# Products of an attention stage cut into half-width pieces for TensorE's array, on one core

## The chip, the cores and the metric

The kernel runs on one core of a Trainium2 chip. The core has TensorE (PE in the profile, its weight loads as PEld), VectorE (DVE), ScalarE (ACT), GpSimd (POOL) and SyncE (SP, which issues DMAs). The metric is the device time of one execution in microseconds. Before the change it is 1563.07 us, the median of three runs (1562.79 to 1563.94).

## The reference

Attention with a decaying state gives x, and x goes through a mixture of eight experts. Per batch b and head h (4 batches, 8 heads, 768 tokens, head size 48):

```
for t in range(S):
    cur   = (u * k[t]) outer v[t]
    y[t]  = r[t] @ (state + cur)
    state = w[:, None] * state + k[t] outer v[t]
x = y, as 3072 tokens x 384
P = exp(x @ w_gate - max), 8 rounds of row and column normalisation
out = sum over e of P[:, e] * (relu(x @ w1[e]) @ w2[e])
```

The inputs are float32. `w1` is 384 x 1024 and `w2` is 1024 x 384 for each expert.

## The kernel before

The first part of the program is a loop over 24 chunks of 128 tokens (`i` in line 733, six chunks to a batch, `c = tt % NCHB`). All of its attention products are float32. For one chunk it holds these stages, each a function:

- `prep` scales r on POOL (`rp`) and k on DVE (`kp`) by tables of powers of w. The heads are stored 64 wide, 48 used and 16 zero, so that two heads (a "pair") fill 128 columns; there are four pairs.
- `stage_b` transposes `rp` and `kp` on PE (`prT`, `pkT`) and ACT copies them out (`rT`, `kT`).
- `stage_c` makes the scores `pA` (eight products, each over 64 of the array's 128 rows), which DVE copies under a mask into `at`; and the chunk's addition to the state, `pu` (four products, `kp` of a pair as weights, 128 x 128, v of the pair streamed, 96 columns). Only the two 48 x 48 blocks on the diagonal of a pair's result are wanted; the table `wbd` holds the decay there and zero elsewhere. DVE adds the old state `S`, and POOL multiplies by `wbd`. The last chunk of a batch has no `pu`, the first one no old state.
- `stage_d` makes y in one PSUM bank `py`: with an old state, four products with `rT` of a pair as weights and `S` streamed (96 columns); then eight, one per head, with `at` as weights and v streamed (48 columns). DVE adds the bonus term (`x`), takes the row's maximum and a power of two as scale.
- `stage_e` and `stage_f` transpose x (`px`), split it into two float16 parts and make the gate's logits.

A float32 product stands as two weight loads and two matmuls in the trace.

The loop is a software pipeline: iteration `i` does `prep(i+2)`, `stage_b(i+1)`, `stage_c(i)`, `stage_e(i-2)`, `stage_d(i-1)`, `stage_f(i-3)`. Every engine takes its instructions in the order in which the program issues them (the class `InOrder`, line 21), so the code fixes the order. Between the stages stand two kinds of filler work. `work(n)` puts in units of the first expert (`ph`: x times w1, `po`: h times w2, float16, split into high and low parts); up to `i = 4` it puts in idle matmuls on zeros (`spin`, `pz`). `prepare()` takes the next step of a list: first the splitting of the first expert's weights (maximum, scale, then a high part on ACT and a low part on DVE, `ws`), later sums of token groups for the other experts (rebuild on DVE, additions on POOL, splitting on ACT and DVE, `xv`). The table `STEPS` (line 721) says for each iteration how many such steps stand ahead of `stage_d` and how many behind it. PSUM tiles of the attention come from `ps3`, four banks with one tag.

After the loop come the remaining units and the other seven experts, where PE does float16 products of up to 512 columns until the end. The change touches nothing there.

Of the kernel before, what the change touches and what calls it, by code (L numbers as in the profile page):

```python
# [8 lines left out]
F32 = mybir.dt.float32  # L9
# [3 lines left out]
ALU = mybir.AluOpType  # L13
# [19 lines left out]
def rwkv_sinkhorn_moe(  # L33
# [30 lines left out]
    HP = 64  # L64
# [204 lines left out]
    ac = att.enter_context(tc.tile_pool(name="ac", bufs=1))  # L269
    ld = att.enter_context(tc.tile_pool(name="ld", bufs=3))  # L270
    at2 = att.enter_context(tc.tile_pool(name="at2", bufs=2))
    ps3 = att.enter_context(tc.tile_pool(name="ps3", bufs=4, space=PSUM))
# [69 lines left out]
    def fill(x_):  # L342
        n = x_.shape[1]
        S_.mul(
            x_.rearrange("p (a q) -> p a q", q=HP),
            unit[:, :1, 1:].broadcast_to([P, n // HP, HP]), 0.0,
        )
# [3 lines left out]
    wbd = ac.tile([P, NPAIR, 2, D], F32, name="wbd")  # L351
# [10 lines left out]
    rp_ = [ac.tile([P, H, HP], F32, name=f"rp{i}") for i in range(2)]  # L362
    kp_ = [ac.tile([P, H, HP], F32, name=f"kp{i}") for i in range(3)]
    at_ = [ac.tile([P, H, C], F32, name=f"at{i}") for i in range(2)]
    for t_ in rp_ + kp_:
        G.memset(t_[:, :, D:], 0.0)
    fill(at_[0].rearrange("p h c -> p (h c)"))

    rk0 = at2.tile([P, H, D], F32, tag="rk", name="rk_0", bufs=3)
# [91 lines left out]
    for j in range(2):  # L461
        rows = slice(j * HP, j * HP + D)
# [61 lines left out]
    def stage_c(tt):  # L524
        d = st[tt]
        c = tt % NCHB
        rT, kT = d["rT"], d["kT"]
        at = at_[tt % 2].rearrange("p (a g) c -> p g a c", g=2)
        pas = []
        for g in range(2):  # L530
            pa = ps3.tile([P, NPAIR, C], F32, tag="pa", name=f"pA_{tt}_{g}")
            pas.append(pa)
        for a in range(NPAIR):
            for g in range(2):
                rows = slice(g * HP, g * HP + HP)
                T.matmul(pas[g][:, a, :], kT[rows, a, :], rT[rows, a, :], start=True, stop=True)
        for g in range(2):
            V.copy_predicated(
                at[:, g], maski.unsqueeze(1).broadcast_to([P, NPAIR, C]), pas[g]
            )  # L540
        if c < NCHB - 1:
            vn = loads[tt]["v"]
            kp = kp_[tt % 3].rearrange("p (a j) d -> p a (j d)", j=2)
            pu = ps3.tile([P, NPAIR, 2 * D], F32, tag="pa", name=f"pu_{tt}")
            for p_ in range(NPAIR):
                T.matmul(
                    pu[:, p_, :], kp[:, p_, :],
                    vn[:, 2 * p_ : 2 * p_ + 2, :].rearrange("p j d -> p (j d)"),
                    start=True, stop=True,
                )  # L550
            sn = at2.tile([P, NPAIR, 2 * D], F32, tag="S", name=f"S_{tt}", bufs=3)
            wb = wbd.rearrange("p a j d -> p a (j d)")
            if c == 0:
                V.tensor_tensor(sn, pu, wb, op=ALU.mult)
            else:
                V.tensor_tensor(sn, pu, d["S"], op=ALU.add)
                G.tensor_tensor(sn, sn, wb, op=ALU.mult)
            st.setdefault(("S", tt + 1), sn)

    def stage_d(tt):  # L560
        d = st[tt]
        c = tt % NCHB
        vn = loads[tt]["v"]
        at = at_[tt % 2]
        py = ps3.tile([P, H, D], F32, tag="pa", name=f"py_{tt}")
        pyp = py.rearrange("p (a j) d -> p a (j d)", j=2)
        first = True
        if c > 0:
            for p_ in range(NPAIR):
                T.matmul(pyp[:, p_, :], d["rT"][:, p_, :], d["S"][:, p_, :], start=first, stop=False)  # L570
                first = False
        for h in range(H):
            T.matmul(py[:, h, :], at[:, h, :], vn[:, h, :], start=first, stop=(h == H - 1))
            first = False
        x = at2.tile([P, DM], F32, tag="x", name=f"x_{tt}")
        V.tensor_tensor(x, py.rearrange("p h d -> p (h d)"), d["av"].rearrange("p h d -> p (h d)"), op=ALU.add)
        m = at2.tile([P, 1], F32, tag="xm", name=f"xm_{tt}")
        V.tensor_reduce(m, x, axis=AX.X, op=ALU.max, apply_absolute_value=True)
        s = at2.tile([P, 1], F32, tag="xs", name=f"xs_{tt}")
        pow2_scale(m, inv_s[:, tt : tt + 1], s, 0.125)  # L580
        d["x"], d["s"] = x, s
# [134 lines left out]
    for sg in range(3):  # L716
# [2 lines left out]
        side += steps  # L719

    STEPS = {
        0: (2, 1), 1: (1, 2), 2: (3, 1), 3: (1, 1),
        4: (1, 1), 5: (1, 1), 6: (2, 1), 7: (1, 1), 8: (1, 1),
    }

    def n_steps(i):
# [6 lines left out]
    for i in range(NTT + 3):  # L733
# [15 lines left out]
        if i < NTT:  # L749
            bonus(i)  # L750
            if ("S", i) in st:
                st[i]["S"] = st.pop(("S", i))
            stage_c(i)
# [17 lines left out]
        if 1 <= i <= NTT:  # L771
            stage_d(i - 1)
# [417 lines left out]
    for s in range(NS):  # L1190
        tasks = stage_tasks(s)
        for g in range(NG):
            for j in range(2):
                for n, nxt in enumerate(g1_slots(s, g, j)):
# [3 lines left out]
                    i = j * NPR + n  # L1198
# [37 lines left out]
```

## Time and profile before

| | |
|---|---|
| median of three runs | 1563.07 us |
| the profiled execution, its own time | 1562.66 us |
| its span | 1561.0 us |
| what lies around the span | 1.66 us |
| granted TensorE clock | 1.00 |
| first row of the loop's iterations to the last y product | about 15 to 257 us |

A row of a group shows the engine, the output and inputs, the tile shapes, the number of instructions, the busy time and the mean of one. `128*128` in a PE row is the part of the array in use, rows by columns. A mean of a matmul is its latency, 270 ns and more; matmuls overlap one another, so what a product costs PE is read from the chain of waits, where the pieces add up without overlap.

### The profile page before, as it was taken

What the parts mean: (1) busy time and instruction counts of PE and PEld (TensorE: products, weight loads), DVE (VectorE), ACT (ScalarE), POOL (GpSimd) and SP (SyncE); (2) the same over time, 40 slices, a digit from 0 to 9 for tenths busy, and PEclk for the clock granted to TensorE, in tenths of its full rate; (3) what the DMA queues carried; (4) which work ended last, traced back from release to release, by engine and by line L of the source; (5) the groups of instructions that cost most, each with busy time, mean ns of one, the idle gap of its engine ahead of it and who ended that gap; (6) DMA issues with size and microseconds to landing.
All of it is one profiled execution on the core that took longest, in us unless ns stands there. A gap on an engine that the chain in (4) does not pass through costs nothing.

```text
span 1561.0 us, 24064 instructions
## 1 busy us (share of the span) xinstructions
PE 1550.4 (99%) x9297; PEld 898.9 (58%) x9297; DVE 1021.1 (65%) x1694; ACT 673.6 (43%) x1192; POOL 581.8 (37%) x686
## 2 busy tenths in 40 slices
PE   8999999999999999999999999999999999999999
PEld 6878776655555555555555555555555555555555
DVE  8876674957666676666676666666666656656554
ACT  4334333534444354544444454544444444535320
POOL 7767764620012424243342424342423324242200
PEclk9999999999999999999999999999999999999999
DMA  9333311221215657576766676665555555556433
GB/s 198 68 87 81 80 51 42 93 79 45 97 60 105 76 86 115 84 127 89 128 87 119 85 127 90 95 96 68 86 57 99 58 94 61 96 59 97 56 91 132
DMA packets 167638, 138.26 MB, mean 89 GB/s; under 512 B 90337, under 2 KB 161762, under 8 KB 167522
## 3 DMA queue, kind: packets, MB, share of 16 engines
q0 software_dynamic: 44928, 61.36, 33.0%
q1 hardware_dynamic: 122384, 75.35, 17.2%
q8 instruction: 73, 1.20, 0.3%
q14 instruction: 43, 0.35, 0.1%
q10 hardware_dynamic: 210, 0.00, 0.0%
HBM read 55.39 MB, written 80.23 MB: 87 GB/s over the span
## 4 chain that ended last, share of the span: by engine, by line
PE 95%; DVE 3%; POOL 0%; issue 0%; ACT 0%; POOLq 0%; DVEq 0%; ACTq 0%
PE po L29 47%; PE bZ L29 11%; PE bY L29 11%; PE ph L29 5%; PE bA L29 5%; PE bB L29 5%; PE py L29 3%; PE bC L29 2%; PE pA L29 1%; PE pu L29 1%; PE px L29 1%; PE prT L29 1%; PE pkT L29 0%; DVE ws L29 0%; POOL rk L29 0%
## 5 line engine op out<-in xcount | busy, mean ns | idle before, releaser
L29 PE MATMUL po<-ws,hbx 128*128 128x384 f16 x3360 | 736.8, 326 | 0.0
L29 POOL DMA_DIRECT2D accd<-stg x288 | 249.7, 867 | 695.8 <-ACT stg L29 677.4
L29 PEld LDWEIGHTS <-hbx 128*128 128x128 f16 x3504 | 336.3, 98 | 292.4 <-issue 0.9
L29 PEld LDWEIGHTS <-ws 128*128 128x128 f16 x3096 | 302.5, 98 | 243.9 <-issue 1.4
L29 ACT ACTIVATE hbx<-tb 128x512 f16<-128x512 f32 x224 | 141.0, 630 | 450.4 <-DVE tb L29 450.4
L29 PE MATMUL po<-ws,hb 128*128 128x384 f16 x1248 | 323.0, 326 | 0.8 <-DVE ws L29 0.8
L29 DVE TENSOR_TENSOR tb<-bY,tb 128x512 f32<-128x512 f32 x168 | 116.2, 692 | 195.7 <-PE bY L29 195.5
L29 ACT ACTIVATE stg<-po,pe 128x384 f32<-128x384 f32 x312 | 179.1, 574 | 121.7 <-PE po L29 96.0
L29 PE MATMUL bZ<-xv,ws 128*128 128x512 f16 x840 | 227.0, 379 | 0.4 <-DVE tb L29 0.4
L29 PE MATMUL bY<-xv,ws 128*128 128x512 f16 x840 | 227.0, 379 | 0.0
L29 DVE TENSOR_TENSOR tb<-bZ,tb 128x512 f32<-128x512 f32 x168 | 115.6, 688 | 136.0 <-PE bZ L29 136.0
L29 PEld LDWEIGHTS <-hb 128*128 128x128 f16 x1248 | 121.8, 98 | 93.9 <-issue 1.0
L29 POOL TENSOR_TENSOR ucb<-rawb 128x256 f32<-128x256 f32 x84 | 76.2, 957 | 117.9 <-DMA rawb<-in_moe_w_dram 117.9
L29 DVE TENSOR_TENSOR tb<-bB,tb 128x512 f32<-128x512 f32 x112 | 77.5, 692 | 48.8 <-PE bB L29 46.9
L29 PE MATMUL ph<-hbx,ws 128*128 128x384 f16 x576 | 104.2, 326 | 0.5 <-DVE hb L29 0.5
L29 DVE SCALAR_TENSOR_TENSOR hb<-tb,hbx 128x512 f16<-128x512 f32 x112 | 77.3, 690 | 24.6 <-ACT hbx L29 19.5
L29 PE MATMUL bA<-xv,ws 128*128 128x512 f16 x336 | 90.8, 379 | 0.0
L29 PE MATMUL bB<-xv,ws 128*128 128x512 f16 x336 | 90.8, 379 | 0.0
L29 DVE SCALAR_TENSOR_TENSOR hbx<-tb,hbx 128x512 f16<-128x512 f32 x112 | 78.0, 696 | 14.7 <-ACT hbx L29 10.4
L29 DVE SCALAR_TENSOR_TENSOR hb<-ph,hb 128x384 f16<-128x384 f32 x64 | 35.4, 554 | 43.5 <-ACT hb L29 43.1
L29 ACT COPY tb<-bZ 128x512 f32<-128x512 f32 x56 | 32.7, 585 | 65.5 <-PE bZ L29 65.5
L29 ACT ACTIVATE hb<-ph 128x384 f16<-128x384 f32 x64 | 31.1, 487 | 62.5 <-PE ph L29 61.6
(168 smaller groups left out, 1608.0 us busy)
## 6 DMA issues: line engine op xcount, KB each, us to landing
accd<-stg POOLq DMA_DIRECT2D x288, 192.0 KB, 3.6
rawb<-in_moe_w_dram SPq DMA_DIRECT2D x28, 768.0 KB, 6.8
e0d<-stg SPq DMA_DIRECT2D x48, 192.0 KB, 1.9
hb<-e0d SPq DMA_DIRECT2D x48, 192.0 KB, 3.8
vn<-in_v_dram SPq DMA_DIRECT2D x24, 192.0 KB, 2.9
accd<-stg SPq DMA_DIRECT2D x24, 192.0 KB, 1.8
accd<-hb POOLq DMA_DIRECT2D x24, 192.0 KB, 4.8
rawb<-accd SPq DMA_DIRECT2D x24, 192.0 KB, 2.4
```

What stands on the lines that cost most here:

```text
L29: return lambda *a, **k: self.tc.keep_in_program_order(f(*a, **k))
```

## The change

Three edits.

1. The products of `stage_d` are made in two halves of 64 tokens. Each half loads 64 weight columns and writes 64 PSUM partitions. Where eight head products and four state products stood, sixteen and eight stand, each as wide in the streamed direction as before.
2. `pu` is made by heads: eight products with 64 columns of `kp` as weights and 48 columns of v streamed; the first head of a pair writes partitions 0 to 63, the second 64 to 127. Off-diagonal blocks are not computed any more, so the state lives in three fixed tiles whose off-diagonal blocks are set to zero once (six POOL memsets at the start), and the DVE and POOL operations on the state are each cut into two, over 64 partitions and 192 elements.
3. `STEPS` changes for iterations 0, 1 and 6.

```diff
+    ss_ = [ac.tile([P, NPAIR, 2, D], F32, name=f"S{i}") for i in range(3)]
...
+    for t_ in ss_:
+        for j in range(2):
+            G.memset(t_[j * HP : (j + 1) * HP, :, 1 - j, :], 0.0)
...
-            pu = ps3.tile([P, NPAIR, 2 * D], F32, tag="pa", name=f"pu_{tt}")
+            pu = ps3.tile([P, NPAIR, D], F32, tag="pa", name=f"pu_{tt}")
             for p_ in range(NPAIR):
-                T.matmul(
-                    pu[:, p_, :], kp[:, p_, :],
-                    vn[:, 2 * p_ : 2 * p_ + 2, :].rearrange("p j d -> p (j d)"),
-                    start=True, stop=True,
-                )
...
+                for j in range(2):
+                    T.matmul(
+                        pu[j * HP : (j + 1) * HP, p_, :], kp[:, p_, j * HP : (j + 1) * HP],
+                        vn[:, 2 * p_ + j, :], start=True, stop=True,
+                    )
+            sn = ss_[tt % 3]
+            for j in range(2):
+                rows = slice(j * HP, (j + 1) * HP)
+                if c == 0:
+                    V.tensor_tensor(sn[rows, :, j, :], pu[rows], wbd[rows, :, j, :], op=ALU.mult)
+                else:
+                    V.tensor_tensor(sn[rows, :, j, :], pu[rows], d["S"][rows, :, j, :], op=ALU.add)
...
+        halves = [slice(i * HP, (i + 1) * HP) for i in range(2)]
...
-                T.matmul(pyp[:, p_, :], d["rT"][:, p_, :], d["S"][:, p_, :], start=first, stop=False)
+                for hs in halves:
+                    T.matmul(
+                        pyp[hs, p_, :], d["rT"][:, p_, hs], d["S"][:, p_].rearrange("p j d -> p (j d)"),
+                        start=first, stop=False, skip_group_check=True,
+                    )
...
-            T.matmul(py[:, h, :], at[:, h, :], vn[:, h, :], start=first, stop=(h == H - 1))
+            for hs in halves:
+                T.matmul(
+                    py[hs, h, :], at[:, h, hs], vn[:, h, :],
+                    start=first, stop=(h == H - 1), skip_group_check=True,
+                )
...
-        0: (2, 1), 1: (1, 2), 2: (3, 1), 3: (1, 1),
-        4: (1, 1), 5: (1, 1), 6: (2, 1), 7: (1, 1), 8: (1, 1),
+        0: (2, 2), 1: (0, 2), 2: (3, 1), 3: (1, 1),
+        4: (1, 1), 5: (1, 1), 6: (2, 2), 7: (1, 1), 8: (1, 1),
```

On PE, in iteration 8, the products of y stand between the transposes of x and the gate's products. `x2` at the end of a row is a count. Before:

```order
L29 MATMUL px_1172<-ident,xsc_1122 128x128 x3
L29 MATMUL py_1180<-S_933,rT_889 128x96 x4
L29 MATMUL py_1180<-vn_583,at_172 128x48 x8
L29 LDWEIGHTS hbx
L29 MATMUL px_1172<-wgp,hbx 128x16
```

And of the changed kernel:

```order
L29 MATMUL px_1297<-ident,xsc_1242 128x128 x3
L29 MATMUL py_1305<-S_173,rT_978 64x96 x8
L29 MATMUL py_1305<-vn_626,at_172 64x48 x16
L29 LDWEIGHTS hbx
L29 MATMUL px_1297<-wgp,hbx 128x16
```

The place is the same; twice as many products, each half as high. `pu` changes in its place too, from `128x96 x4` to `64x48 x8`.

On DVE, in iterations 7 and 8, the rows with `ws_75` are the low parts of the first expert's second weight, in three pieces. Before, iteration 7 ends and iteration 8 goes on like this:

```order
L29 RECIPROCAL xs_1085<-inv_s 128x1
L29 TENSOR_SCALAR lparts<-px_1062,inv_s,iswg 128x16
...
L29 TENSOR_TENSOR S_1157<-pu_1152,S_1047 128x384
...
L29 TENSOR_TENSOR hbx<-px_1172,hbx 128x3x128
L29 SCALAR_TENSOR_TENSOR ws_75<-ws_74,sw_309,ws_75 128x1024
L29 TENSOR_TENSOR x_1193<-py_1180,rk_881 128x384
...
L29 RECIPROCAL xs_1197<-inv_s 128x1
L29 SCALAR_TENSOR_TENSOR ws_75<-ws_74,sw_309,ws_75 128x1024
```

Of the changed kernel:

```order
L29 RECIPROCAL xs_1204<-inv_s 128x1
L29 SCALAR_TENSOR_TENSOR ws_75<-ws_74,sw_318,ws_75 128x1024
L29 TENSOR_SCALAR lparts<-px_1176,inv_s,iswg 128x16
...
L29 TENSOR_TENSOR S_175<-pu_1272,S_174 64x4x48 x2
...
L29 TENSOR_TENSOR hbx<-px_1297,hbx 128x3x128
L29 SCALAR_TENSOR_TENSOR ws_75<-ws_74,sw_318,ws_75 128x1024
L29 TENSOR_TENSOR x_1330<-py_1305,rk_970 128x384
...
L29 RECIPROCAL xs_1334<-inv_s 128x1
L29 SCALAR_TENSOR_TENSOR ws_75<-ws_74,sw_318,ws_75 128x1024
```

The first piece moved from iteration 8 to the end of 7, the second from behind the x chain of iteration 8 to ahead of it, and the third from iteration 9 into 8.

On DVE, in iterations 0 and 1, `wma` is the maximum over the first expert's first weight, which PE then transposes (`pmax_w`). Before:

```order
L29 TENSOR_REDUCE wm_310<-ws_74 128x1 x3
L29 TENSOR_REDUCE wgm<-wg 128x1
...
L29 TENSOR_SCALAR md_wg<-ident,mt_wg 1x1
L29 TENSOR_REDUCE wma_0_311<-wm_310 128x1
L29 TENSOR_TENSOR x_466<-py_457,rk_179 128x384
```

Of the changed kernel:

```order
L29 TENSOR_REDUCE wm_319<-ws_74 128x1 x3
L29 TENSOR_REDUCE wma_0_320<-wm_319 128x1
L29 TENSOR_REDUCE wgm<-wg 128x1
...
L29 TENSOR_SCALAR md_wg<-ident,mt_wg 1x1
L29 TENSOR_TENSOR x_492<-py_475,rk_188 128x384
```

It moved from behind iteration 1's mask copies to iteration 0. The order on SP is the same in both kernels. On ACT one high part moved a place forward; on POOL, beside the memsets and the cut state operations, one token sum in some iterations.

More of the change, by code (lines that the diff above doesn't have):

```diff
@@ L543, in stage_c @@
             kp = kp_[tt % 3].rearrange("p (a j) d -> p a (j d)", j=2)
-            pu = ps3.tile([P, NPAIR, 2 * D], F32, tag="pa", name=f"pu_{tt}")
+            pu = ps3.tile([P, NPAIR, D], F32, tag="pa", name=f"pu_{tt}")
             for p_ in range(NPAIR):
-                T.matmul(
-                    pu[:, p_, :], kp[:, p_, :],
-                    vn[:, 2 * p_ : 2 * p_ + 2, :].rearrange("p j d -> p (j d)"),
-                    start=True, stop=True,
-                )
[L551 to L557, printed above, removed]
+                for j in range(2):
[10 more added lines that the diff above has]
+                    V.tensor_tensor(sn[rows, :, j, :], pu[rows], d["S"][rows, :, j, :], op=ALU.add)
+            if c:
+                for j in range(2):
+                    rows = slice(j * HP, (j + 1) * HP)
+                    G.tensor_tensor(
+                        sn[rows, :, j, :], sn[rows, :, j, :], wbd[rows, :, j, :], op=ALU.mult
+                    )
             st.setdefault(("S", tt + 1), sn)
@@ L569, in stage_d @@
             for p_ in range(NPAIR):
-                T.matmul(pyp[:, p_, :], d["rT"][:, p_, :], d["S"][:, p_, :], start=first, stop=False)
+                for hs in halves:
[3 more added lines that the diff above has]
+                    )
                 first = False
         for h in range(H):
-            T.matmul(py[:, h, :], at[:, h, :], vn[:, h, :], start=first, stop=(h == H - 1))
+            for hs in halves:
+                T.matmul(
+                    py[hs, h, :], at[:, h, hs], vn[:, h, :],
+                    start=first, stop=(h == H - 1), skip_group_check=True,
+                )
             first = False
```

## The prediction

> **What bounds the kernel now.** I read the page first, then busy times by stretches, then the chain of waits inside the loop, then groups by shape.
>
> ```profile
> span 1561.0 us, 24064 instructions
> PE 1550.4 (99%) x9297; PEld 898.9 (58%) x9297; DVE 1021.1 (65%) x1694; ACT 673.6 (43%) x1192; POOL 581.8 (37%) x686
> PE 95%; DVE 3%; POOL 0%; issue 0%; ACT 0%; POOLq 0%; DVEq 0%; ACTq 0%
> ```
>
> PE ends last nearly everywhere. The change touches the loop alone, so I cut the span there (up to 59 us; up to the first expert's late weights; the rest of the loop; after it):
>
> ```profile
> 0.00:59.00 59.00, 54.16 (x428) 40.67 (x429) 51.82 (x100) 23.93 (x36) 46.81 (x55) 1.00 0.73 155
> 59.00:88.50 29.50, 28.78 (x258) 23.62 (x257) 25.27 (x57) 13.94 (x24) 18.43 (x19) 1.00 0.35 68
> 88.50:257.40 168.90, 168.83 (x1444) 132.97 (x1444) 110.67 (x223) 58.10 (x113) 117.06 (x130) 1.00 0.29 69
> 257.40:1561.00 1303.60, 1298.65 (x7174) 701.68 (x7170) 833.32 (x1318) 577.65 (x1019) 399.47 (x483) 1.00 0.53 89
> ```
>
> The columns are length, then busy PE, PEld, DVE, ACT, POOL. From 59 us on PE is full, while DVE (110.67 of 168.90) and POOL (117.06) have a third to spare. A microsecond taken from PE between 59 and 257 us should come off the end. Up to 59 us PE also runs idle matmuls on zeros, and DVE sets the pace.
>
> The chain over one loop iteration gives prices that add up, each piece from the end of the one before:
>
> ```profile
> 166.38 1.09 PE pA L29 x16
> 167.47 1.06 PE pu L29 x8
> 168.53 1.95 PE po L29 x12
> 170.48 1.46 PE ph L29 x9
> 171.94 0.33 PE px L29 x3
> 172.27 2.61 PE py L29 x24
> 174.88 0.13 PE px L29 x6
> ...
> 177.41 1.09 PE pA L29 x16
> 178.50 2.06 PE po L29 x12
> ...
> 204.90 1.72 PE py L29 x16
> ```
>
> The last row is a chunk without old state: its sixteen matmuls of `at` and v take 1.72 us, 107.5 ns each. So the eight with `S` cost 2.61 - 1.72 = 0.89 us, 111 ns each. One streams 48 columns, the other 96, yet they cost the same: **the 128-column weight load sets the pace, not the stream.**
>
> **The change part by part.**
>
> ```profile
> L29 PE MATMUL py<-vn,at 128*128 128x48 f32 x304 | 36.3, 273 | 0.0
> L29 PE MATMUL pA<-rT,kT 64*128 64x128 f32 x288 | 20.9, 285 | 0.0
> L29 PE MATMUL pu<-vn,kp 128*128 128x96 f32 x120 | 17.0, 284 | 0.0
> L29 PE MATMUL py<-S,rT 128*128 128x96 f32 x128 | 16.5, 272 | 0.0
> L29 PEld LDWEIGHTS py<-vn,at 128*128 128x128 f32 x304 | 35.5, 192 | 0.0
> L29 PEld LDWEIGHTS pmax_w<-ident,wma 128*1 128x1 f32 x1 | 0.1, 84 | 0.0
> ```
>
> These are the groups from 59 to 258 us. At 16, 8 and 8 matmuls a visit they are 304/16 = 19 y products of v, 128/8 = 16 of the state, and 120/8 = 15 of `pu`.
>
> *Pace of a pair of halves.* Nothing before splits the array by columns, but `pA` splits it by rows: sixteen matmuls in 1.09 us, 68 ns each with the switch included, against 107.5 to 111 ns on the whole array. So two halves do run at one time. A load's time also falls with its columns: 84 ns for one column, 192 ns for 128 (latencies). If a 64-column load takes half of 107.5 ns and the two halves load together, a pair goes by in 54 ns. Bounds: six gate matmuls take 0.13 us, 22 ns for each load with its product, so two can't be issued faster than 43 ns; if the halves take turns, a pair costs the old 107.5 ns. I take 54, since the row split is the nearest row. The stream of the state's product then counts:
>
> ```profile
> 281.04 0.49 PE L29 MATMUL pc<-pm,ones 128*128 128x192 f32 x2
> 281.37 0.65 PE L29 MATMUL ph<-hbx,ws 128*128 128x384 f16 x3
> ```
>
> Two float32 matmuls of 192 columns take 0.33 us from start to start, 0.86 ns a column; 96 columns need 82 ns (bounds 54 and 111), 48 columns 41, hidden under the load.
>
> - v product: 16 pairs x 54 = 0.86 us for 1.72: -0.86, times 19 = -16.3.
> - state product in y: 8 x 82 = 0.66 for 0.89: -0.23, times 16 = -3.7.
> - `pu`: of its 1.06, 8 x 111 = 0.89 is pace and the rest the switch from `pA`, which stays. After: 8 x 54 = 0.43: -0.46, times 15 = -6.9.
>
> *Switches.* Into `pA`: 1.09 - 8 x 0.111 = 0.20 us beyond its pace. Out of it: the twelve `po` behind `pA` take 2.06, elsewhere 1.95: 0.11. Now py has a switch in and out (0.31 x 19 = +5.9) and `pu` one out (0.11 x 15 = +1.7). A column split might switch more cheaply, down to nothing, or at twice that; I take the row split's price.
>
> Sum on PE: -26.9 + 7.6 = **-19.3 us**.
>
> *The weight steps.* Before, five matmuls of the first `po` wait for a low part:
>
> ```profile
> 88.57 0.97 PE L29 MATMUL po<-ws,hb 128*128 128x384 f16 x5 [0.79 <-DVE ws L29]
> 84.14 1.51 DVE L29 SCALAR_TENSOR_TENSOR ws<-ws,sw,ws 128x1024 f16<-128x1024 f32 x1
> 87.26 1.26 DVE L29 SCALAR_TENSOR_TENSOR ws<-ws,sw,ws 128x1024 f16<-128x1024 f32 x1
> ```
>
> The second of these pieces moves to the place of the first, ahead of the x chain, so the wait goes: **-0.8**. But a third piece comes into iteration 8. DVE had 29.50 - 25.27 = 4.2 us free between 59 and 88.5; PE now wants to be 4 us earlier there, and DVE gets about 1.3 more. What is late next is `at` or `hbx` in iterations 8 and 9. Most of it lies in the one-iteration distance between mask copy and y; I charge **+1.0** (0 to 2.5).
>
> *State on DVE and POOL.*
>
> ```profile
> L29 DVE TENSOR_TENSOR S<-pu,S 128x384 f32<-128x384 f32 x16 | 8.7, 543 | 0.0
> L29 DVE COPY wbd<-wc 48x192 f32<-48x192 f32 x2 | 0.5, 254 | 0.1
> L29 DVE TENSOR_TENSOR logits<-lparts 128x192 f32<-128x192 f32 x1 | 0.4, 359 | 0.0
> L29 POOL TENSOR_TENSOR ws<-ws 128x256 f32<-128x256 f32 x51 | 36.2, 725 | 1.5
> L29 POOL TENSOR_TENSOR S<-S,wbd 128x384 f32<-128x384 f32 x16 | 16.0, 998 | 1.2 <-DVE S L29 1.2
> ```
>
> A DVE half lies between the copy and the sum of 192 columns, so two take 0.51 to 0.72 us: +0.1. On POOL, 128 columns more cost 273 ns (725 to 998), so a half is about 0.59: +0.2 a chunk. Both lie under PE from 59 us on. The six memsets come before POOL's wait of 5.19 us for the first table, and hide:
>
> ```profile
> 12.11 2.28 POOL L29 TENSOR_TENSOR rp<-rn,rtab 128x384 f32<-128x384 f32 x2 [5.19 <-ACT rtab L29]
> 177.00:187.50 10.50, 10.50 (x92) 8.09 (x91) 5.96 (x14) 4.61 (x9) 9.49 (x11) 1.00 0.40 90
> ```
>
> The second row is the iteration in which POOL is fullest: 9.49 us. PE falls there from 10.5 to 9.7 (no `pu`): still just over POOL. I charge **+0.5** (0 to 2) for such iterations.
>
> *Up to 59 us.* PE no longer waits for the maximum `wma`, and py gets shorter:
>
> ```profile
> 25.88 0.27 PE L29 MATMUL pmax_w<-ident,wma 128*1 128x128 f32 x1 [0.94 <-DVE wma L29]
> 34.39 0.56 DVE L29 TENSOR_TENSOR x<-py,rk 128x384 f32<-128x384 f32 x1 [0.71 <-PE py L29]
> ```
>
> DVE gains only its own waits (this 0.71 and about 0.9 in two smaller ones), and pays 0.1 per state: **-0.5** (-1.6 to +0.7).
>
> Sum: -19.3 - 0.8 + 1.0 + 0.5 - 0.5 = -19.1. The profiled execution took 1562.66 us (span 1561.0 and 1.66 around it), 0.4 under the median. 1562.66 - 19.1 = 1543.6; on the median's scale 1544.0. I give **1543.8**.
>
> **The rivals.**
>
> *A, the halves take turns (slower).* If two column halves share one path for weights and stream, loads gain nothing: v and `pu` pairs stay at 107.5 ns, a state pair streams 2 x 82 = 164 for 111 (+0.42 x 16 = +6.8), and the switches stay. +6.8 + 7.6 - 0.8 = +13.6: 1576. It decides from a pair time of 96 ns: 424 pairs (19 x 16 + 15 x 8) at 107.5 - 96 and 128 at 111 - 96 give 6.8, which the net of switches and wait (7.6 - 0.8) eats. For it: both halves read the same 128 partitions, where `pA`'s halves read different ones. Against it: in the gate's rows a float16 load of 128 columns with its product goes by in 22 ns, so weights can enter far faster than 128 float32 columns in 107.5.
>
> *B, a half's load waits while the other half streams.* Then a pair is 2 x (54 + 41) = 190 ns for v and `pu`, 2 x (54 + 82) = 272 for the state: 424 x 0.08 + 128 x 0.16 = +55, with switches and wait +62: 1625. Against it: whole-array loads now go by at 107.5 ns under matmuls of 273 ns latency on the same rows. The Trainium skill, "TensorE: Matmul & The Clock Gate", "The mechanism", states this rule: a weight load overlaps with matmuls in flight only where its row group differs. This trace shows the overlap without any such difference, so I give the rule little.
>
> *C, the halves overlap in part.* At `pA`'s gross 68 ns a pair: v -0.63 x 19 = -12.0, `pu` -0.35 x 15 = -5.2, state -3.7, switches and wait +6.8: -14; with less to catch up on, no charge for DVE and POOL: 1549. The Trainium skill, "TensorE: Matmul & The Clock Gate", "Measured speedup vs the span model", has three column tiles at 2.38 times one; two at that share (1.59) would be an estimated 68 ns as well, and the same sum. No run here shows it.
>
> *D, POOL or DVE becomes the bound.* Of the seventeen iterations from 60.9 to 241.4 us, eight have POOL busy for 8.0 us or more; the first and the last of them:
>
> ```profile
> 100.60:112.10 11.50, 11.50 (x100) 9.09 (x99) 9.36 (x20) 4.02 (x8) 8.85 (x11) 1.00 0.56 141
> 208.70:220.20 11.50, 11.50 (x100) 9.10 (x99) 7.95 (x19) 4.97 (x9) 8.02 (x9) 1.00 0.10 36
> ```
>
> If these keep their old length because POOL also waits for DVE, eight times 1.1 us is lost: +9, 1552. Against it: POOL's tiles are prepared one to two iterations ahead.
>
> *E, the steps don't do their part:* the 0.8 us wait stays. It lies inside the forecast's range.
>
> **How the numbers follow.** Forecast 0.58: its ends are 1537 (state pairs at 54, no charges, the early gain) and 1548 (all three charges at their dear ends); switches twice as dear would reach 1555. C 0.12, D 0.10, A 0.14, B 0.03; 0.03 for faster than 1536, if switches cost nothing. The range 1536 to 1556 holds the forecast, C and D, 0.80. A measurement here tells 0.2%, 3.1 us, from no change. Forecast, C, D and the cheap end give 0.83, A and B 0.17. Of these I put 0.05 within 0.2%, for a pair time near 96 ns: 0.02 from C, 0.03 from A. So faster is 0.81, slower 0.14.
>
> **What would show it.** In the profile after: the chain's py at about 1.7 us in place of 2.61 (0.66 + 0.86 + 0.20 for the switch in), `pu` near 0.6, the `po` or `ph` behind `pu` 0.11 longer; the two halves' weight loads in pairs; no wait of `po` for `ws` at the first expert; iterations about 1.1 us shorter. A shows as py of 3 us or more, D as PE waiting for POOL or DVE between 90 and 250 us. Idle PE time in the loop over 3 us, or a py above 2.4 us, would make the prediction wrong.

## The result, and the profile after

The changed kernel takes **1547.69 us** (median of 4 runs, 1546.85 to 1548.8) against 1563.04 (4 runs, 1562.79 to 1563.94). The ratio is 0.9901, with a 95% interval of 0.9884 to 0.9918. It is faster, as forecast, and 3.9 us slower than the forecast of 1543.8. The profiled execution took 1547.53 us with a span of 1545.8.

The page of the changed kernel: span, and each engine's share of the chain that ended last.

```profile
span 1545.8 us, 25532 instructions
...
PE 91%; DVE 4%; POOL 2%; ACT 1%; issue 1%; DMA 0%; POOLq 0%; ACTq 0%; DVEq 0%
```

PE's share of the chain fell from 95% to 91%, and POOL, ACT and issue came in. So the shorter products are not all of the story: somewhere PE now waits. Busy times by stretches (length, then PE, PEld, DVE, ACT, POOL; the third figure from the end is the granted clock) say where:

```profile
0.00:59.00 59.00, 49.85 (x570) 34.20 (x570) 52.91 (x103) 23.74 (x35) 48.04 (x64) 0.97 0.72 155
59.00:88.50 29.50, 27.46 (x370) 21.19 (x368) 26.96 (x61) 14.04 (x26) 20.95 (x23) 1.00 0.35 69
88.50:243.00 154.50, 152.12 (x1905) 112.39 (x1904) 110.16 (x235) 57.78 (x113) 121.77 (x140) 1.00 0.32 75
```

PE was idle for 4.8 us of the first 59 before and is for 9.2 now, and its clock there is 0.97 in place of 1.00. In the long stretch of the loop it was idle for 0.07 us in all, and now is for 2.4.

Where the chain runs on PE, an iteration shows what the halves do. Pieces of the chain of waits in iterations 14 and 15 (start, length, what):

```profile
144.01 1.73 PE py L29 x48
145.74 0.24 PE px L29 x6
...
148.85 1.09 PE pA L29 x16
149.95 0.60 PE pu L29 x16
150.55 1.57 PE ph L29 x9
```

The products of y take 1.73 us for 2.61, `pu` 0.60 for 1.06. The pieces behind them, `px` and `ph`, are 0.11 longer each (0.13 to 0.24, 1.46 to 1.57): that is the switch out of column mode. Groups by shape from 59 to 243 us:

```profile
L29 PE MATMUL po<-ws,hb 128*128 128x384 f16 x269 | 47.4, 326 | 0.0
L29 PEld LDWEIGHTS py<-vn,at 128*64 128x64 f32 x610 | 19.9, 138 | 0.5 <-issue 0.5
L29 POOL TENSOR_TENSOR S<-S,wbd 64x192 f32<-64x192 f32 x24 | 14.1, 588 | 0.9
L29 DVE TENSOR_TENSOR S<-pu,S 64x192 f32<-64x192 f32 x24 | 8.4, 348 | 0.4
```

A load of 64 columns takes 138 ns for 192. `po` no longer waits for a weight (0.0 in the last column). The last two rows are halves of the state's update: two cost 1.18 us on POOL (998 ns before) and 0.70 on DVE (543 ns before).

The start of `pA` in each iteration shows where time is won and lost. The first two columns are before and after; the other two are experiments told below.

| iteration | before | after | zero_late_step9 | z9_compact |
|---|---|---|---|---|
| 0 | 14.98 | 15.68 | 16.02 | 15.14 |
| 3 | 35.82 | 34.36 | 33.38 | 33.12 |
| 4 | 43.27 | 44.79 | 43.24 | 43.54 |
| 5 | 52.52 | 54.38 | 53.02 | 51.13 |
| 9 | 89.47 | 88.10 | 86.75 | 84.26 |
| 11 | 112.51 | 108.87 | 107.52 | 105.03 |
| 12 | 122.59 | 118.96 | 116.82 | 114.34 |
| 17 | 177.34 | 168.58 | 166.82 | 163.95 |
| 18 | 187.90 | 179.63 | 176.69 | 173.74 |
| 23 | 241.74 | 228.29 | 225.35 | 222.40 |
| span | 1561.0 | 1545.8 | 1542.8 | 1540.6 |

Three things stand out. At iteration 5 the changed kernel is 1.86 us **behind**, where the prediction had it 0.5 ahead. From there it gains 17.06 to the end. And iterations 11 and 17 gain nothing or lose: 10.08 to 10.09 us, and 10.56 to 11.05.

**The early loss.** It has a first part on DVE and POOL. Before, in order of time (POOL's row, then DVE's):

```profile
5.93 0.99 POOL L29 TENSOR_TENSOR rk<-rn,kn 128x384 f32<-128x384 f32 x1
8.13 0.14 DVE L29 TENSOR_TENSOR good<-wt,wsafe 128x4 f32<-128x4 f32 x1
```

And after:

```profile
5.91 1.78 POOL L29 MEMSET S<- 64x192 f32 x6
7.78 1.25 POOL L29 TENSOR_TENSOR rk<-rn,kn 128x384 f32<-128x384 f32 x1
8.15 0.90 DVE L29 TENSOR_TENSOR good<-wt,wsafe 128x4 f32<-128x4 f32 x1
```

The memsets push `rk` to 7.78, and DVE's little `good`, due at 8.15, lasts until `rk` ends at 9.03. The decay table hangs on `good`, and the first `pA` is 0.7 us later. A second part is on PE. Before and after, PE in iteration 3 (idle time ahead of a row in brackets):

```profile
35.82 1.16 PE L29 MATMUL pA<-rT,kT 64*128 64x128 f32 x16
36.91 1.13 PE L29 MATMUL pu<-vn,kp 128*128 128x96 f32 x8
```

```profile
34.36 0.48 PE L29 MATMUL pA<-rT,kT 64*128 64x128 f32 x2
35.83 1.16 PE L29 MATMUL pA<-rT,kT 64*128 64x128 f32 x14 [0.98 <-DVE x L29]
38.07 1.09 PE L29 MATMUL pu<-vn,kp 128*64 128x48 f32 x16 [1.08 <-ACT rT L29]
39.09 1.46 PE L29 MATMUL pz<-zeros 128*128 128x512 f16 x3
```

PE comes 1.46 us sooner, waits twice, and then runs slowly: `pu` takes 1.09 us where the same row takes 0.67 at full clock, three fillers 1.46 for 0.81. The granted clock over 5 us each:

```profile
35.00:40.00 5.00, 3.09 (x33) 2.26 (x34) 4.83 (x10) 3.66 (x5) 3.82 (x3) 0.80 1.03 192
40.00:45.00 5.00, 5.00 (x72) 3.86 (x72) 4.90 (x9) 2.60 (x4) 4.41 (x5) 0.86 0.46 81
```

In the profile of before it is 1.00 in every 5 us. (The column leaves out the slow start: it gives 1.00 from 0 to 5 us too, where the fillers run at half their later pace in every profile.) Of the length of iteration 3 the waits make the larger part. In zero_late_step9, an experiment below, PE waits as long in iteration 3, and its clock there is 1.00:

```profile
34.86 1.16 PE L29 MATMUL pA<-rT,kT 64*128 64x128 f32 x14 [1.00 <-DVE x L29]
37.10 0.67 PE L29 MATMUL pu<-vn,kp 128*64 128x48 f32 x16 [1.08 <-ACT rT L29]
```

Iteration 3 still takes 9.86 us there, against 10.43 in the changed kernel and 7.45 before.

**Iterations 11 and 17.** At the end of iteration 9 and the start of 10, DVE's rebuild of a weight and POOL's rows, then PE in iteration 11:

```profile
98.64 0.94 DVE L29 TENSOR_TENSOR ws<-hbx 128x768 f32<-128x768 f16 x1
...
99.74 1.08 POOL L29 TENSOR_TENSOR ws<-ws 128x256 f32<-128x256 f32 x1 [5.77 <-DMA e0d<-stg]
100.79 1.00 POOL L29 TENSOR_TENSOR rp<-rn,rtab 128x384 f32<-128x384 f32 x1
...
116.35 0.29 PE L29 MATMUL px<-wgp,hbx 128*128 128x16 f16 x6 [0.74 <-DVE hbx L29]
```

POOL stands idle for 5.77 us ahead of a token sum. A DMA is named as what ended it, but DVE's rebuild, on which the sum depends, ends at 99.58, 0.16 us before. Behind the sum in POOL's order stands `rp`, which needs nothing of it. Before, `rp` ran right behind the state:

```profile
93.48 1.00 POOL L29 TENSOR_TENSOR rp<-rn,rtab 128x384 f32<-128x384 f32 x1
```

So the moved weight steps put a waiting sum ahead of ready work; POOL then has no gap from 100.79 to past 115, and the chain goes through it to ACT's and DVE's `hbx` and to PE. The same stands ahead of iteration 17: POOL idle for 6.43 us before the sum at 159.99, and PE waiting 1.22 us for `hbx` at 176.53.

### The profile page after: what moved, and what is told of

Its sections match the earlier page's. It is cut to its first block, busy times and chain, and to the rows that moved or that the text cites. A ratio compares the mean times of both kernels' runs of the same rounds, so it can differ in the third digit from the quotient of the medians.

```text
span 1545.8 us, 25532 instructions
## 1 busy us (share of the span) xinstructions
PE 1527.4 (99%) x10001; PEld 869.1 (56%) x10001; DVE 1022.6 (66%) x1714; ACT 673.8 (44%) x1192; POOL 590.3 (38%) x708
## 4 chain that ended last, share of the span: by engine, by line
PE 91%; DVE 4%; POOL 2%; ACT 1%; issue 1%; DMA 0%; POOLq 0%; ACTq 0%; DVEq 0%
PE po L29 47%; PE bZ L29 12%; PE bY L29 12%; PE bA L29 5%; PE bB L29 5%; PE ph L29 4%; PE bC L29 2%; PE py L29 1%; POOL rk L29 1%; PE pA L29 1%; PE px L29 1%; DVE ws L29 1%; PE prT L29 0%; POOL ws L29 0%; DVE hbx L29 0%
```

## The experiments

All were timed against the kernel before, which took 1562.96 to 1563.1 us in the four sets of runs.

### turns: do the halves need to alternate?

```diff
-            for p_ in range(NPAIR):
-                for hs in halves:
+            for hs in halves:
+                for p_ in range(NPAIR):
...
-        for h in range(H):
-            for hs in halves:
+        for hs in halves:
+            for h in range(H):
```

The same in `pu`; the same products, only all of the first half ahead of all of the second.

> All products of the first half come ahead of all of the second (y and the state's product), nothing else changes. Theory (two halves run at one time, a pair of loads in 56 ns): in turn each 64-column load takes its own 56 ns and each 96-column stream about 82, so per visit v goes from 0.87 to about 1.8 us, the old state's product from 0.68 to about 1.3, pu from 0.45 to 0.9: 19 x 0.9 + 16 x 0.65 + 15 x 0.45 = +34 us, about 1582. Rival (the gain comes from shorter loads alone, the order of halves does not matter): 1547.7.

Measured: 1563.19 us (10 runs), ratio 1.0001 (0.9991 to 1.0011). The gain of the whole change is gone. In the chain of waits an iteration has:

```profile
161.61 2.58 PE py L29 x47
...
167.91 0.87 PE pu L29 x16
```

2.58 in place of 1.73, and 0.87 in place of 0.60. Against the whole products (2.61 and 1.06) that is a little less, and the two switches out take it up. So fewer columns and smaller products bring nothing in sum by themselves: **the gain is the overlap of the two halves**, and it is had in full only if they alternate in the program. The loss is less than turns throughout would give (1582). PE's rows in order of time show why:

```profile
150.81 0.26 PE L29 MATMUL py<-vn,at 128*64 128x48 f32 x1
150.88 0.25 PE L29 MATMUL py<-S,rT 128*64 128x96 f32 x1
150.90 0.28 PE L29 MATMUL py<-vn,at 128*64 128x48 f32 x2
```

The program has all sixteen of `S` ahead of all of v. On the chip some products of v start ahead of the last of `S`. By the program's order those of v are of the first half and those of `S` of the second; the rows themselves don't name the half. So over a distance of a few instructions each half seems to run as a queue of its own.

### steps_old: the weight steps alone undone

```diff
-        0: (2, 2), 1: (0, 2), 2: (3, 1), 3: (1, 1),
-        4: (1, 1), 5: (1, 1), 6: (2, 2), 7: (1, 1), 8: (1, 1),
+        0: (2, 1), 1: (1, 2), 2: (3, 1), 3: (1, 1),
+        4: (1, 1), 5: (1, 1), 6: (2, 1), 7: (1, 1), 8: (1, 1),
```

> The changed kernel with the old table of steps. Theory (the new table lets POOL's first token sum stand ahead of rp, where it waits for DVE; iterations 11 and 17 lose 0.8 and 1.3 us by it): those 2.1 us come back, and the first po waits again for the low part of the weights, 0.8 us and up to 1.6 more since PE is earlier: between 1546 and 1549. Rival (the new table only helps): 1549.5 or more, with iterations 11 and 17 as long as now.

Measured: 1546.88 us (1546.31 to 1547.38), ratio 0.9896 (0.988 to 0.9913), which its runs don't tell from the change. Two effects of like size cancel. The wait of `po` for a weight is back, longer than the 0.79 us it was, and `rp` is back behind the state:

```profile
88.18 0.97 PE L29 MATMUL po<-ws,hb 128*128 128x384 f16 x5 [1.40 <-DVE ws L29]
...
93.28 0.99 POOL L29 TENSOR_TENSOR rp<-rn,rtab 128x384 f32<-128x384 f32 x1
```

Iteration 11 takes 9.29 us and iteration 17 9.90, iteration 8 10.00 for 8.83. The steps do remove the wait; they pay it back on POOL.

### zero_late and zero_late_step9: the two losses one at a time

zero_late moves the six memsets behind `rk`; zero_late_step9 also holds one step of iteration 9 back, so that the shifted sum no longer stands ahead of `rp`.

```diff
-    for t_ in ss_:
-        for j in range(2):
-            G.memset(t_[j * HP : (j + 1) * HP, :, 1 - j, :], 0.0)
...
     G.tensor_tensor(rk0, loads[0]["r"], loads[0]["k"], op=ALU.mult)
+    for t_ in ss_:
+        for j in range(2):
+            G.memset(t_[j * HP : (j + 1) * HP, :, 1 - j, :], 0.0)
...
-        4: (1, 1), 5: (1, 1), 6: (2, 2), 7: (1, 1), 8: (1, 1),
+        4: (1, 1), 5: (1, 1), 6: (2, 2), 7: (1, 1), 8: (1, 1), 9: (2, 1),
```

> The six memsets of the state tiles stand behind POOL's first product rk instead of ahead of it. Theory (the memsets push rk under DVE's comparison good, which then takes 0.90 us instead of 0.14, at the head of DVE's chain): good is back at 0.14 us, the first pA starts at 15.0 us instead of 15.7, and the total falls by about 0.7 us to 1547.0. Rival (the memsets collide with DVE there too, or the 0.7 is lost again before 59 us): no change.

> As zero_late, and iteration 9 takes one step less behind stage_d (2, 1), so that from iteration 10 on the order on POOL is that of before, while the low parts of the weights stay where the change has put them. Theory: POOL no longer waits with a token sum ahead of rp, iterations 11 and 17 fall to about 9.3 and 9.8 us, -2.1 us beside the -0.7: about 1545. Rival (POOL is late there because the state's two half operations take 0.25 us more): iterations 11 and 17 stay, 1547.

Measured: zero_late 1547.10 us (1546.76 to 1548.21), ratio 0.99 (0.9884 to 0.9917); zero_late_step9 1545.26 (1544.56 to 1545.58), ratio 0.9888 (0.9871 to 0.9904). With the memsets behind `rk`, in zero_late:

```profile
6.88 1.75 POOL L29 MEMSET S<- 64x192 f32 x6
8.22 0.14 DVE L29 TENSOR_TENSOR good<-wt,wsafe 128x4 f32<-128x4 f32 x1
```

The first `pA` starts at 15.13 for 15.68; the 0.6 us in the medians lies inside the spread of the runs, and in the profile the gain is lost again by iteration 5 (55.40 for 54.38, with a clock of 0.66 from 50 to 55 us). `good` is back at 0.14 us though the memsets run beside it: it was `rk` that held it, not the memsets. The Trainium skill, "SBUF — State Buffer", "Who interferes with whom", says that a VectorE instruction with two SBUF inputs contends with a GpSimd instruction that reads SBUF, not with one that only writes it. `good` has two inputs, `rk` reads and a memset writes: the trace agrees, 0.90 and 0.14 us.

The one held step is worth 1.84 us in the medians, and the ranges of the runs don't meet. Iterations 11 and 17 take 9.30 and 9.87 us in the profile of zero_late_step9, for 10.09 and 11.05. The cause of that loss is settled.

### y_only and state_split: the two halves of the change apart

y_only is the kernel before with y's halves and the new steps; state_split is the kernel before with the fixed zeroed tiles and the update in two halves of 64 rows, and nothing else (all products whole).

```diff
y_only:
-                T.matmul(pyp[:, p_, :], d["rT"][:, p_, :], d["S"][:, p_, :], start=first, stop=False)
+                for hs in halves:
+                    T.matmul(
+                        pyp[hs, p_, :], d["rT"][:, p_, hs], d["S"][:, p_, :],
+                        start=first, stop=False, skip_group_check=True,
+                    )
...
state_split:
-            sn = at2.tile([P, NPAIR, 2 * D], F32, tag="S", name=f"S_{tt}", bufs=3)
+            sn = ss_[tt % 3]
+            for j in range(2):
+                rows = slice(j * HP, (j + 1) * HP)
...
+                    V.tensor_tensor(sn[rows, :, j, :], pu[rows, :, j * D : (j + 1) * D], d["S"][rows, :, j, :], op=ALU.add)
```

> The kernel before with y's products alone in halves and the new weight steps; the state's product and its update stay whole, and nothing is zeroed for it. Theory (the gain of y's halves is 1.2 us less 0.3 us of switches in each of 19 visits, and the state's halves bring 0.35 us in each of 15 iterations, about 5.2 us, while the zeroing and the split update cost some 1.5 us in the first 60 us): 1547.7 + 5.2 - 1.5 = about 1551.4 us, an iteration of the steady part 10.25 us against 9.90, the first 60 us about 1.5 us shorter than with the whole change. Rival (the split update also costs where TensorE is behind, on VectorE or GpSimd, so that the state's halves bring nothing in sum): 1547 to 1548.5 us.

> The kernel before with whole products and the old weight steps, but with the state in three fixed tiles that are zeroed at the start and its update in two halves of 64 rows on VectorE and GpSimd. Theory (the zeroing pushes GpSimd's rk under VectorE's good, 0.7 us, and each half pair on VectorE costs 0.18 us more and on GpSimd 0.25 us in the some 5 iterations that wait for them): 1564.0 to 1565 us, 1 to 2 us over before, all of it in the first 60 us. Rival (the early iterations have slack for it, and the early loss comes of the shorter products and the clock): 1563.1 us, within 0.4.

Measured: y_only 1548.60 us (1547.86 to 1549.12), ratio 0.9907 (0.9893 to 0.9921); state_split 1566.30 (11 runs, 1564.78 to 1566.55), ratio 1.0018 (1.0009 to 1.0028).

y_only is 2.8 us below the theory (1551.4) and 0.1 above the range of the rival, which came nearer. The theory's sum left out that the changed kernel, and not this one, is late in iterations 11 and 17 (by 0.79 and 0.89 us between the two profiles). The state's halves do bring what they should where PE sets the pace: an iteration is 10.25 us there against 9.90, since `pu` takes 1.06 again:

```profile
149.34 1.06 PE pu L29 x8
...
154.14 1.73 PE py L29 x48
```

But y_only is at iteration 5 at 52.52 us, 1.86 ahead of the change. In iteration 11 it takes 9.30 us, although POOL waits there as in the change:

```profile
98.48 1.11 POOL L29 TENSOR_TENSOR ws<-ws 128x256 f32<-128x256 f32 x1 [5.91 <-DVE ws L29]
```

So the loss came with both, the shifted sum and the state's halves. That the wait is made good here because iterations are longer on PE and the state is whole on POOL is argued; no run parts the two. By these numbers **the state's product in halves brings some 5 us in the loop (15 times 0.35), and what comes with it gives some 4 back**; 0.9 us in the medians is left.

state_split costs 3.3 us, more than the 1 to 2 of the theory. At iteration 5 it is 3.84 us behind before (56.36 for 52.52), and from iteration 7 on by 3.4 to 3.7. Part of that is the clock, as its windows show:

```profile
10.00:15.00 5.00, 3.52 (x14) 2.58 (x15) 2.85 (x8) 1.57 (x3) 1.73 (x2) 0.66 0.98 212
50.00:55.00 5.00, 4.22 (x30) 3.55 (x30) 4.80 (x12) 1.27 (x3) 4.69 (x7) 0.72 0.20 39
```

Its runs fall in two groups, four of 1564.8 to 1565.3 and seven of 1566.3 to 1566.6. What the split costs without the clock was left for z9_compact.

### z9_spin5 and z9_fill25: is it the clock?

Both start from zero_late_step9. The first makes each filler stretch of the early iterations five products long, the second the very first stretch six longer.

```diff
z9_spin5:
-            spin(3)
+            spin(5)
z9_fill25:
-    spin(19)
+    spin(25)
```

> Zeroing behind rk and two steps at iteration 9 as in zero_late_step9, and in the early iterations each filler stretch of TensorE made of 5 filler products in place of 3. Theory (TensorE, with shorter products, idles more in the first 60 us, and the granted clock that falls there to 0.80 to 0.86 costs about 1 us and spreads the runs): the clock stays at 1.00 in every 5 us of the first 60, 1544.3 us against 1545.3, and a narrower range. Rival (the fillers stand in front of products that are ready, and delay them): 1545.3 to 1546.5 us with the clock at 1.00.

> zero_late_step9 with 25 filler products at the very start of TensorE in place of 19. Theory (the early runs differ because the clock rises from the 0.427 us step of a filler to the 0.216 us step at a moment of its own, 4.3 to 7.3 us after the start; where it rises early the fillers end early, TensorE stands 2.5 to 3.3 us before the table product, and the clock is at half for 3.5 us from about 11.3, which makes the first pA 0.9 us late): six more fillers, 1.3 us, close that gap; the first pA at about 15.1 us and the clock at 1.00 in every 5 us, 1544.4 us, the range narrower. Rival (the fall does not hang on that gap): 1545.3 us, with 0.66 between 10 and 15 us still in the profile.

Measured: z9_spin5 1545.37 us (1545.07 to 1545.8), ratio 0.9887 (0.9871 to 0.9903): no gain, as its rival said; in its profile the clock is 1.00 from 15 us on, but so it is in that of zero_late_step9, so this run says little of the clock. z9_fill25 1545.54 (1545.17 to 1546.85), ratio 0.9893 (0.9876 to 0.9909): no gain. PE's first rows in state_split and in z9_fill25:

```profile
1.31 6.86 PE L29 MATMUL pz<-zeros 128*128 128x512 f16 x24 [1.31 <-DVE zeros L29]
11.48 1.94 PE L29 MATMUL pt_tab<-ident,hb 128*128 128x128 f32 x8 [3.31 <-DVE wc L29]
```

```profile
1.32 8.88 PE L29 MATMUL pz<-zeros 128*128 128x512 f16 x30 [1.32 <-DVE zeros L29]
10.87 1.06 PE L29 MATMUL pt_tab<-ident,hb 128*128 128x128 f32 x8 [0.68 <-DVE wc L29]
```

In state_split a wait of 3.31 us stands ahead of the table product, and it runs at half speed (1.94 for 1.06). In z9_fill25 the wait is 0.68, the product runs at full speed, and the first `pA` comes at 15.14 (16.02 in zero_late_step9). All fourteen profiles agree: the clock is low there in the four with a wait of 2.50 to 3.31 us (state_split, y_only, zero_late_step9, z9_spin5), and not in the ten with 0.59 to 2.05. That the six added fillers made the difference isn't shown, though: with 19 at the start the wait is also short where the fillers sped up late (1.55 us in z9_compact). And in z9_fill25 the clock falls in iteration 3 instead (0.66 from 35 to 45 us), behind waits of 1.94 and 1.08 us, and iteration 3 takes 12.51 us.

### z9_compact, z9c_fill25: the update in one instruction

z9_compact keeps the state as 128x192, so that DVE and POOL update it whole, and ACT spreads it into one of two fixed block tiles for y.

```diff
+            sn = at2.tile([P, NPAIR, D], F32, tag="S", name=f"Sc_{tt}", bufs=3)
...
+                V.tensor_tensor(sn, pu, d["S"], op=ALU.add)
+                G.tensor_tensor(sn, sn, wbc, op=ALU.mult)
...
+        if i < NTT and i % NCHB:
+            for j in range(2):
+                S_.copy(ss_[i % 2][j * HP : (j + 1) * HP, :, j, :], st[i]["S"][j * HP : (j + 1) * HP])
```

> zero_late_step9 with the state kept as 128x192, so that VectorE and GpSimd update it in one instruction each, and ScalarE copies the two halves of 64 rows into one of two fixed block tiles before y's products of the next iteration. Theory (the update in two halves costs about 1.3 us of the first 60, as state_split without the zeroing and the clock showed): 1544.0 us against 1545.3, the gain all before iteration 6. Rival (ScalarE's two copies stand ahead of its rT and kT copies in the early iterations and delay TensorE): 1545 to 1547 us.

> z9_compact and z9_fill25 together. Theory: both gains add up, 1543.1 us. Rival: one of them gives nothing, 1544 to 1545 us.

Measured: z9_compact **1543.11 us** (1542.1 to 1544.22), ratio 0.9877 (0.986 to 0.9893), 2.15 under zero_late_step9, whose runs all lie above its own; z9c_fill25, the same with 25 fillers at the start, 1543.71 (1542.77 to 1544.09), ratio 0.9877 (0.986 to 0.9893): the two gains don't add up, and in its profile iteration 3 takes 12.75 us for 10.42. The groups up to 59 us, of z9_compact:

```profile
L29 ACT COPY S<-Sc 64x192 f32<-64x192 f32 x10 | 3.5, 347 | 0.1
L29 POOL TENSOR_TENSOR Sc<-Sc,wbc 128x192 f32<-128x192 f32 x4 | 2.4, 592 | 0.0
L29 DVE TENSOR_TENSOR Sc<-pu,Sc 128x192 f32<-128x192 f32 x4 | 1.4, 339 | 0.0
```

One update of 128 rows takes 339 ns on DVE and 592 on POOL, no more than a half of 64 rows did (348 and 588). The ACT copies, 0.7 us a chunk, are not free. In iteration 3 they stand between two weight pieces and `rT`, as the rival said (ACT's rows, then PE's):

```profile
34.30 0.71 ACT L29 COPY S<-Sc 64x192 f32<-64x192 f32 x2
36.08 0.56 ACT L29 COPY rT<-prT 128x512 f32<-128x512 f32 x1
36.70 0.67 PE L29 MATMUL pu<-vn,kp 128*64 128x48 f32 x16 [1.83 <-ACT rT L29]
```

In zero_late_step9 that wait was 1.08, but one of 1.00 for DVE's `x` came before it, so `pu` isn't later here. The gain is more than the 1.3 us of the theory. In the profiles z9_compact is 1.89 us ahead by iteration 5, of which 0.88 stand already at the first `pA`, where zero_late_step9 had its slow clock. What is left for the update up to iteration 5 is about 1.0, with another 0.6 by iteration 9; this is a subtraction between two profiles whose clocks fall in different places.

### z9c_gap and z9c_fill25_gap: filling the wait of iteration 3

```diff
+        if tt == 3:
+            spin(8)
         for g in range(2):
             V.copy_predicated(
```

> z9_compact with 8 filler products of TensorE in iteration 3 between pA and pu, where it waits 1.83 us for ScalarE's rT (ScalarE first scales two weight pieces). Theory (that idle time makes the clock fall: in z9_compact the granted clock is 0.74 and 0.91 from 35 to 45 us, and iterations 3 and 4 take 10.42 and 7.59): 8 fillers at the 0.216 us step, 1.7 us, fit into the wait and hold the clock at 1.00; iteration 3 about 9.4 us, 1542.0 us against 1543.1. Rival (the clock falls for another reason, or the fillers delay pu): the same 1543.1 us or up to 0.5 more.

> z9c_fill25 (25 fillers at the start) with the same 8 fillers in iteration 3, where the clock was 0.68 and 0.64 from 35 to 45 us and iteration 3 took 12.75 us. Theory: with both gaps filled the clock is at 1.00 in all of the first 60 us, iteration 3 is 9.5 to 10.5 us, 1541.5 us, and the runs lie within 0.8 us of each other. Rival: no change against z9c_fill25, 1543.7 us.

Measured: z9c_gap 1542.78 us (1542.25 to 1544.08), ratio 0.9867 (0.9851 to 0.9884); z9c_fill25_gap 1542.65 (1542.44 to 1543.23), ratio 0.9869 (0.9852 to 0.9885). The window of z9c_gap in which the clock was lowest without the fillers:

```profile
35.00:40.00 5.00, 4.62 (x44) 2.82 (x44) 4.86 (x8) 4.26 (x7) 3.83 (x3) 1.00 1.09 197
```

The clock stays at 1.00 in both profiles in every 5 us of the first 60, and with both gaps filled the runs lie within 0.8 us. This fits the idea that idle time lets the clock fall, but one profile of each doesn't show it: zero_late_step9 had no fillers in iteration 3, waited there too, and kept its clock. The gain is small as well: 0.3 and 1.1 us against the same kernel without the fillers, where the ranges of the runs overlap. And the clock isn't what makes iteration 3 long: in the profile of z9c_gap it took 10.45 us at full clock, as much as in z9_compact with a low one, since a wait stood ahead of the fillers, inside `pA`,

```profile
35.38 1.16 PE L29 MATMUL pA<-rT,kT 64*128 64x128 f32 x14 [1.32 <-DVE x L29]
```

which z9c_fill25_gap did not have (iteration 3: 8.98). What makes DVE's `x` late in some executions stays open: in this profile POOL had stood 1.47 us for something on SP's queue around 20 us, which was not tried. The last two kernels are the fastest here, 20.3 and 20.5 us under the kernel before, but not told apart from z9_compact by these runs.

## Why the prediction was right, and where it was not

**What bounds the kernel: right for the products, not for the whole loop.** The pace of the products of y was set by the 128-column load, and two 64-column loads run side by side. turns shows that this overlap is the whole gain. What didn't hold is that PE stays full, so that all it saves comes off the end: from 59 to 243 us PE was idle for 0.8 us before and is for 4.4 now, and the prediction itself had named 3 us of idle PE in the loop as a sign against it.

**The PE sum: right, in part by luck.** For y the prediction had 1.72 us, and the chain shows 1.73; for `pu` 0.60 and 0.60; the pieces behind are 0.11 longer, as forecast. Within y two small errors cancel. By their single starts from 59 to 243 us, a pair of v takes 58 or 59 ns where 54 were forecast, 0.06 us more in a visit. The switch into y takes 0.14 us where 0.20 were forecast: behind `px` the first product starts 0.09 later than it did before, and the first pair of the state takes 0.05 more than the others. A steady iteration went from 11.03 to 9.90 us, which is the forecast's -0.86 - 0.23 - 0.46 + 0.31 + 0.11 = -1.13. The row split of `pA` was a good measure for a column split, in the overlap and in the switch out.

**The weight steps: the wait went as forecast** (iteration 8: 10.51 to 8.83 us). Of the charge of 1.0 for DVE in iterations 8 and 9 little shows there: iteration 8 is 1.68 shorter where 1.13 and 0.8 were to come off, with a wait of 0.34 for DVE's `hbx`, and iteration 9 is 1.14 shorter.

**POOL: the step that failed.** The prediction took 0.5 us from a comparison of busy times ("PE falls there from 10.5 to 9.7 (no `pu`): still just over POOL"). It named one of the two iterations, 17, and its range to 2 held the price: 1.84 us by the held step. But the cause is not that POOL is too full. The step of the weights moved a token sum ahead of `rp`, and an engine that works in order stood idle for 5.77 us with ready work behind. The prediction counted what the moved step does for DVE and PE, and not what it moves on POOL, although the section on the change notes that a token sum moves there.

**Up to 59 us: a term mis-sized, -0.5 forecast and +1.86 measured.** Of its parts:
- The memsets "hide" before POOL's wait for the first table: they don't, since `rk` stands behind them and lands on DVE's `good`; the first `pA` is 0.70 later than before, and 0.55 of that goes in zero_late. The wait that should have hidden them came after the row that they push.
- The state's update "+0.1" on DVE and "+0.2" on POOL: in the first 59 us two halves take 2 x 347 ns on DVE for 542, and 2 x 702 ns on POOL for 1002. Undoing it brought 2.15 us in the medians, of which the profiles leave some 1.0 to the update up to iteration 5. The estimate from sizes (a half between a copy and a sum of 192 columns) put the halves' sum at 0.51 to 0.72 us, and they took the dear end: here time goes with the elements of a row, not with the rows (339 ns for 128x192, 348 for 64x192).
- What y and `pu` themselves gain there was about right: z9_compact, without these costs, is 1.39 us ahead of before at iteration 5, inside the forecast's -1.6 to +0.7.
- Not thought of at all: the clock, which fell in iteration 3. Its share is small beside the waits: iteration 3 takes 10.43 us with the low clock and 9.86 in zero_late_step9 without.

With these taken away, z9_compact is at 1543.1 us, 0.7 from the forecast. From iteration 5 to the end zero_late_step9 gains 18.70 us, against a forecast of -19.3 - 0.8 + 1.0 + 0.5 = -18.6. The charge for POOL is gone there with the held step. The one for DVE is found in other places than forecast: PE waits for DVE in iterations 6, 7, 8, 13, 16 and 19, 0.19 to 0.34 us each and 1.66 in all, in five of them for `hbx`. So that charge had the right mechanism and was too small, and the 0.5 for POOL, which doesn't occur there, happens to make it up: that the sum is so close is luck.

**The rivals.** By single starts, a pair of v goes by in 58 or 59 ns and a pair of the state in 82 or 83 (forecast 54 and 82). That puts out A (107.5), B (190) and C (68). The rule behind B, of the Trainium skill, "TensorE: Matmul & The Clock Gate", "The mechanism", doesn't hold here: the two halves' loads are over the same 128 rows, and overlap. D was right in its place and its mechanism (PE waits for POOL in the loop, by way of ACT and DVE), and small: two iterations, not eight.

## What to carry to other kernels

Two column halves of TensorE pay if they alternate in the program and the weight load sets the pace; price them by the load of half the columns, and the mode's switch by a row split in the same trace. On VectorE and GpSimd an instruction over 64 rows took as long as one over 128 rows of the same length, so don't cut such an instruction into row halves to match: keep the operands compact and let an engine with time to spare spread them. When a step is moved, read the order on every engine that it issues to: an engine waits in order, and a sum that is early there can hold up work that was ready.

## What the runs showed of the hardware

- **Two column halves, one pace.** Two 64-column loads with 48 columns of stream go by as a pair in 58 or 59 ns, where one 128-column load took 107.5.
- **Halves as queues of their own.** With all of one half ahead of the other in the program, products of v started ahead of state products that stand before them in the program (turns, rows at 150.81 to 150.90); by the program's order they are of different halves.
- **Rows cost nothing at these sizes.** 64x192 and 128x192 take the same time: 348 and 339 ns on VectorE, 588 and 592 on GpSimd.
- **The clock rises and falls on a schedule of its own.** The same 24 fillers took 8.30 us in one execution and 6.86 in another. Read one by one, they start 0.427 us apart at first and 0.216 later, and the pace changes at 7.3 us in the profile of before and at 4.7 in that of zero_late_step9. There PE was then idle for 2.58 us; the pace fell back at 11.3 us and was up again by 15.2. The slow spells behind it come in one size: in the windows of 5 us the clock's shortfall adds up to about 3.4 us at half clock (0.80 and 0.86 in the changed kernel, 0.66 in zero_late_step9), or twice that (0.66 and 0.66 in z9_fill25). The Trainium skill, "TensorE: Matmul & The Clock Gate", "What's actually happening", puts the decision on windows of about 3.4 us that run free of the kernel: the trace agrees on both, a varying moment and spells of that length. Waits well under 3.4 us stood ahead of a fall: 0.98 and 1.08 us in iteration 3 of the changed kernel, with 1.16 us of products between. The same waits (1.00 and 1.08) in zero_late_step9 were followed by none, so their length alone doesn't decide.
- **A small instruction held.** `good`, 0.14 us of work, took 0.90 while GpSimd's `rk` was running.
